# Reciprocal row sums of the first batch spread over 64 rows by TensorE transposes, and x of a pair formed one iteration sooner

## The chip, the cores and the metric

The kernel runs on one core of a Trainium2 chip. The metric is the device time of one execution in microseconds (us): the median of the runs. Before the change it is 807.39 us, the median of three runs from 806.12 to 808.97. For this kernel a difference of about 0.3% (2.4 us) is the least that can be told from no change.

## What is computed

The reference chains three blocks in float32: causal attention (4 batches, 12 heads, 448 tokens, 64 numbers per head), a gated block with a causal convolution of 5 taps, and a block with sine and cosine.

```python
scores = scale * q @ k.T ; masked above the diagonal
attn   = exp(scores - max)
attn   = attn / (attn.sum(-1) + 1e-9)
x      = attn @ v                         # heads side by side: (4, 448, 768)

gate   = 1 / (1 + exp(-conv5(x, conv_w)))
x      = (gate * (x @ w_val)) @ w_out

theta  = x @ w_theta
y      = w_tok_r @ (x * cos(theta)) + w_tok_i @ (x * sin(theta))
u      = x + y
out    = u + max(u @ w_ch, 0)
```

## The kernel before

**Attention, one iteration per head.** `attn_iter(i)` runs head i in five segments; two heads are a pair g, and each batch has six pairs. An iteration computes the scores of four row blocks (L320, L321: "S"), the row maxima on VectorE (L322), the exponentials on ScalarE (L116, with the row sums as a by-product), and in the iteration after it the transposes of the probabilities (L341) and their copies out of PSUM (L354). After both heads of a pair, TensorE multiplies by v (L364: "AV"), without having divided by the row sums. At the end of every odd iteration q and k of the next pair are transposed (L283) and split into a high and a low half (L298 to L308). No S of the next pair can start before these splits: below, this stretch is the boundary between two pairs.

**The division.** `attn_R` forms the reciprocals of the row sums, a tile `rec` of 112 rows x 8 (L379, L380). They are needed along the columns and equal on all 64 rows of a head. So `rec` is written to memory (`rows<-rec`, L382), and two DMAs read it back, each spreading a head's 448 numbers over 64 rows (`rb<-rows`, L397). All of these are issued from SyncE's queue, in order with every other load and store. `attn_X1` then forms x of the pair on VectorE, `xf = av * rb` (L408), splits it on ScalarE (`x_hi`, L413) and on GpSimd (`x_lo`, L108), and `attn_X2` runs the convolution (L423 to L430 on GpSimd) and the gate. In iterations, pair g is attended in 2g and 2g+1, its AV and its read-back stand at the end of iteration 2g+2, and `attn_X(g)` stands near the end of iteration 2g+3.

**The first batch.** There is no dense work beside the attention of batch 0. Its loop (L664) runs 69 segments: batch 0 and nearly two heads of batch 1. Beside it run the preparation of the first weight tiles (`to_f32` on VectorE: L153, L156, L160; splits on GpSimd: L105, L108) and, for two output tiles, the first dense product ahead of time: `gemm_ahead(kc)`, six 448-column matmuls per pair (L451), which reads `x_hi` and `x_lo` of pair kc. After it, `dense(b)` is interleaved with the attention of the next batch by a table of rates (L694 to L699).

**What sets the order.** Each engine runs its own list in order; a waiting instruction holds all behind it. A scheduler with a model of the times made the lists when the program was built. PSUM has 2 buffers for dense products and 6 for all else. `issue_after` keeps `xf` behind the last row maximum that was written before it in the code.

```python
seg(n): if j == 1 and n == (X_LAST if g == NP else X_SEG): attn_X(g - 1)   # L617, both 3
...
if AHEAD and i >= 4 and i % 2 == 0 and c == A_SEG and i // 2 - 2 < KC - 1:  # L678
    gemm_ahead(i // 2 - 2)
```

Of the kernel before, what the change touches and what calls it, by code (L numbers as in the profile page):

```python
# [9 lines left out]
F32 = mybir.dt.float32  # L10
# [11 lines left out]
ROUND = 12582912.0  # L22

X_SEG = 3
X_LAST = 3
U_DVE = (0, 1, 1, 1)
PT_DVE = (2, 2, 0, 0)
K_DUP = (2, 2, 2, 2, 2, 2, 0, 0, 0, 0, 0, 0, 0, 0, 0, 1, 0, 1, 0, 0, 0, 0, 0, 0)
# [5 lines left out]
AHEAD = 2  # L34
A_SEG = 2
# [14 lines left out]
def kernel(  # L50
# [14 lines left out]
    nc = tc.nc  # L65
    B, H, S, D = q.shape
    DM = H * D
    P = 128
    CP = 112
    NC = S // CP  # L70
    NP = H // 2
    KC = DM // P
# [8 lines left out]
    pool = ctx.enter_context(tc.tile_pool(name="pool", bufs=2))  # L81
# [18 lines left out]
    def psum(tag):  # L100
        at = "mm" if tag == "mm" else "at"
        return ps.tile([P, 512], F32, tag=at, name=f"ps_{tag}", bufs=2 if tag == "mm" else 6)
# [145 lines left out]
    gates = {}  # L248
    rbs = {}
    row_at = {}  # L250
    ttr_ins = []
    hf_ins = []

# [103 lines left out]
    def attn_AV(g):  # L357
        if not 0 <= g < B * NP:
            return
        tv = v_raw.pop(g)  # L360
        av[g] = psum("av")
        for kc in range(NC):
            for j in range(2):
                nc.tensor.matmul(  # L364
                    av[g][j * D : (j + 1) * D, kc * CP : S], lhsT=tv[:, j, kc, :], rhs=pT.pop((2 * g + j, kc)),
                    start=kc == 0, stop=kc == NC - 1, skip_group_check=True,
                )

    def attn_X(g):
        if not 0 <= g < B * NP:  # L370
            return
        attn_X1(g)
        attn_X2(g)

    def attn_R(g):
        if not 0 <= g < B * NP:
            return
        rec = pool.tile([CP, 2, NC], F32, tag="rec", name="rec")
        nc.vector.tensor_scalar(out=rec, in0=sums[g], scalar1=1.0e-9, scalar2=None, op0=ALU.add)  # L379
        nc.vector.reciprocal(rec, rec)  # L380
        rows = dram.tile([2, NC, CP], F32, tag="rows", name="rows", bufs=2)
        nc.sync.dma_start(out=rows.rearrange("h c p -> p h c"), in_=rec)  # L382
        row_at[g] = rows

    def attn_B(g):
        if g not in row_at:
            return
        rows = row_at.pop(g)
        with ExitStack() as st:
            if g + 2 in v_ins:  # L390
                st.enter_context(tc.issue_after(v_ins[g + 2].ins))
            attn_B2(g, rows)
# [50 lines left out]
    def gemm_ahead(kc):  # L443
        xhi, xlo = x_hl[0, kc]
        g = kc // KH
        for n in range(AHEAD):
            if kc == 0:
                ahead[n] = psum("mm" if n < 2 else "tr")
            whi, wlo = splits[n, g]
            for m, (a, x) in enumerate(((whi, xhi), (whi, xlo), (wlo, xhi))):  # L450
                nc.tensor.matmul(  # L451
                    ahead[n][:, :S], lhsT=a[:, kc % KH, :], rhs=x,
                    start=kc == 0 and m == 0, stop=kc == KC - 1 and m == 2, skip_group_check=True,
                )
            if kc == KC - 1:
                splits.pop((n, 0)), splits.pop((n, 1))
# [156 lines left out]
    def attn_iter(i):  # L613
        g, j = divmod(i, 2)

        def seg(n):
            if j == 1 and n == (X_LAST if g == NP else X_SEG):  # L617
                attn_X(g - 1)

        attn_PT(i - 1, (0,))  # L620
        attn_S(i, 0)
        seg(0)
        yield
        attn_PT(i - 1, (1,))
        attn_S(i, 1)
        seg(1)
        yield
        attn_PT(i - 1, (2, 3))
        attn_S(i, 2)
        seg(2)  # L630
        yield
        attn_S(i, 3)
        attn_T(i + 1)
        if j == 1:
            load_qk(g + 3, "q")
            load_qk(g + 3, "k")
            attn_R(g)
        seg(3)
        yield
        if j == 0:  # L640
            attn_AV(g - 1)
            load_v(g + 1)
            attn_B(g - 1)
        if i == B * H:
            attn_X(g - 1)
        seg(4)
        yield
# [16 lines left out]
    for n in range(5 * (H + 1) + X_SEG + 1):  # L664
        next(at, None)
        if n == 5:
            setup_conv()
        if W_AT <= n < 5 * H:
            with tc.issue_after(ttr_ins[-1].ins):
                for at_n, (m, g) in zip(A_TILES, ((0, 0), (1, 0), (0, 1), (1, 1), (2, 0), (2, 1), (3, 0), (3, 1))):  # L670
                    if n == at_n - W_AT:
                        load_w(m, g)
                    if n == at_n:
                        stage_w(m, g)
                        if m < AHEAD + 1:
                            split_w(m, g)
        i, c = divmod(n, 5)
        if AHEAD and i >= 4 and i % 2 == 0 and c == A_SEG and i // 2 - 2 < KC - 1:  # L678
            gemm_ahead(i // 2 - 2)
        if n == 5 * H - 3:  # L680
            with tc.issue_after(ttr_ins[-1].ins):
                for g in range(2):
                    load_w(AHEAD + 2, g)
    if AHEAD:
        gemm_ahead(KC - 1)
    for b in range(B):
        done = 0
        for y, _ in enumerate(dense(b)):
# [44 lines left out]
```

## Time and profile before

| | |
|---|---|
| median of 3 runs | 807.39 us |
| profiled execution, whole | 811.03 us |
| its span, first to last instruction | 809.2 us |
| TensorE busy | 725.1 us, 90% |
| VectorE busy | 493.8 us, 61% |
| ScalarE busy | 427.4 us, 53% |
| GpSimd busy | 316.2 us, 39% |
| mean granted TensorE clock | 0.949 of 2.4 GHz |

These are means over stages that differ. The attention of batch 0 by itself lasts to about 122 us; there no engine is busy throughout, and the TensorE clock is granted at its lower level (0.50: 1.2 GHz) for part of the time. From 122 to about 262 us VectorE is nearly always busy, and after that TensorE is. So the profile is read stage by stage.

### The profile page before, as it was taken

The page shows a single profiled execution, that of the slowest core. Times are in us where ns is not written, and L with a number is a line of the kernel's source. Part 1 is how long each engine was busy: PE and PEld are TensorE (multiplying, and loading weights), DVE is VectorE, ACT ScalarE, POOL GpSimd, SP SyncE. Part 2 cuts the span into 40 slices and gives each one's busy share as a digit, 9 for nine tenths or more (in the row PEclk, how much of TensorE's full clock was granted, in tenths as well). Part 3 has the DMA queues.
Part 4 walks back from the last instruction along what each step waited for, and adds up shares of the span by engine and source line. Part 5 has one row for each costly group of instructions (what it writes and reads, how often), then busy time and mean ns, then how long its engine had stood idle before and what let it go on. Part 6 is the DMA issues. An engine that isn't in the chain of part 4 may idle for free.

```text
span 809.2 us, 11956 instructions
## 1 busy us (share of the span) xinstructions
PE 725.1 (90%) x3965; PEld 609.7 (75%) x3965; DVE 493.8 (61%) x1125; ACT 427.4 (53%) x998; POOL 316.2 (39%) x327
## 2 busy tenths in 40 slices
PE   5687889698598798999989899899999998999997
PEld 4455558577387686788978788788888787988996
DVE  4666869999999837535657645653666732114541
ACT  6767754465567744435687633444787622124401
POOL 0386976586355658123226610113234232201100
PEclk9888779789699999999999999999999999999999
DMA  9548627979576248778744259579824078774323
GB/s 233 125 104 182 151 47 200 236 238 294 142 221 140 63 133 225 225 234 184 157 136 86 60 144 190 148 221 196 178 58 102 12 140 215 214 212 139 98 57 90
DMA packets 151850, 126.01 MB, mean 156 GB/s; under 512 B 93519, under 2 KB 126829, under 8 KB 151789
## 3 DMA queue, kind: packets, MB, share of 16 engines
q1 hardware_dynamic: 151789, 125.25, 60.9%
q8 instruction: 31, 0.51, 0.3%
q14 instruction: 30, 0.25, 0.1%
HBM read 100.76 MB, written 24.47 MB: 155 GB/s over the span
## 4 chain that ended last, share of the span: by engine, by line
PE 54%; DVE 18%; DMA 9%; ACT 8%; POOL 6%; issue 4%; SPq 1%; ACTq 0%; POOLq 0%; DVEq 0%
PE ps_mm L472 28%; PE ps_mm L567 10%; PE ps_av L364 5%; PE ps_tr L341 3%; PE ps_s L320 2%; DVE gate L434 2%; PE ps_s L321 2%; DMA out_dram<-o 2%; DVE cv_raw L156 2%; DMA rb<-rows 2%; DMA scratch<-w_hl 2%; POOL gate L430 2%; DVE qs L111 1%; DMA rows<-rec 1%; ACT prob L116 1%
## 5 line engine op out<-in xcount | busy, mean ns | idle before, releaser
L472 PE MATMUL ps_mm<-act_hi,w_hl 128*128 128x448 f32 x864 | 274.1, 379 | 10.7 <-POOL w_hl L105 7.0
L472 PEld LDWEIGHTS ps_mm<-act_hi,w_hl 128*128 128x128 f32 x864 | 165.1, 193 | 27.9 <-POOL w_hl L105 9.4
L472 PE MATMUL ps_mm<-act_lo,w_hl 128*128 128x448 f32 x432 | 160.4, 373 | 0.0
L116 ACT ACTIVATE prob<-ps_s,negm 112x112 f32<-112x112 f32 x192 | 95.4, 498 | 71.4 <-DVE negm L322 69.4
L322 DVE CUSTOM_DVE_ANT_0 ps_s<-ps_s,mask 112x112 f32<-112x112 f32 x192 | 86.2, 454 | 76.3 <-PE ps_s L321 62.6
L320 PE MATMUL ps_s<-kk,qs 128*112 128x256 f32 x192 | 73.9, 389 | 21.3 <-DVE qs L111 4.8
L341 PE MATMUL ps_tr<-ident,prob 112*112 112x112 f32 x480 | 80.4, 271 | 13.2 <-ACT prob L116 7.6
L108 POOL TENSOR_TENSOR act_lo<-x2f,act_hi 128x448 fp32r<-128x448 f32 x36 | 43.9, 1218 | 119.8 <-ACT act_hi L486 57.0
L472 PEld LDWEIGHTS ps_mm<-act_lo,w_hl 128*128 128x128 f32 x432 | 83.4, 194 | 5.0
L354 ACT COPY pt<-ps_tr 112x448 f32<-112x448 f32 (+2 forms) x120 | 51.5, 440 | 60.7 <-PE ps_tr L341 60.2
L472 PE MATMUL ps_mm<-x_hi,w_hl 128*128 128x448 f32 x264 | 80.5, 374 | 2.3 <-ACT x_hi L413 1.1
L341 PEld LDWEIGHTS ps_tr<-ident,prob 112*112 112x112 f32 x480 | 57.3, 138 | 28.0 <-ACT prob L116 11.7
L567 PE MATMUL ps_mm<-wtok_h,zt_h 128*128 128x448 f32 x168 | 64.2, 382 | 5.6 <-ACT zt_h L558 5.6
L567 PE MATMUL ps_mm<-wtok_h,zt_l 128*128 128x448 f32 x168 | 63.6, 378 | 1.3 <-DVE zt_l L111 1.1
L321 PE MATMUL ps_s<-klo,qs 128*112 128x256 f32 x192 | 63.0, 339 | 1.4 <-DVE klo L111 1.4
L364 PE MATMUL ps_av<-pt,v_raw 112*64 112x224 f32 (+3 forms) x384 | 63.3, 446 | 0.9 <-ACT prob L116 0.8
L567 PE MATMUL ps_mm<-wtok_l,zt_h 128*128 128x448 f32 x168 | 62.3, 371 | 0.0
L320 PEld LDWEIGHTS ps_s<-kk,qs 128*112 128x112 f32 x192 | 36.6, 192 | 30.0 <-ACT kk L307 6.5
L430 POOL TENSOR_TENSOR gate<-gate,tp 128x448 f32<-128x448 f32 x48 | 57.8, 1205 | 2.8
L108 POOL TENSOR_TENSOR x_lo<-xf,x_hi 128x448 fp32r<-128x448 f32 x23 | 29.4, 1279 | 74.5 <-ACT x_hi L413 74.1
L543 POOL TENSOR_TENSOR z<-z,x2f 128x448 f32<-128x448 f32 x18 | 20.9, 1160 | 92.3 <-ACT z L540 92.3
L472 PEld LDWEIGHTS ps_mm<-x_hi,w_hl 128*128 128x128 f32 x264 | 50.3, 191 | 8.6 <-DVE hf L510 2.2
(97 smaller groups left out, 1362.0 us busy)
## 6 DMA issues: line engine op xcount, KB each, us to landing
w_hl<-scratch SPq DMA_DIRECT2D x144, 384.0 KB, 3.9
scratch<-w_hl SPq DMA_DIRECT2D x44, 384.0 KB, 4.2
q_raw<-in_q_dram SPq DMA_DIRECT2D x48, 112.0 KB, 3.6
k_raw<-in_k_dram SPq DMA_DIRECT2D x48, 112.0 KB, 3.3
v_raw<-in_v_dram SPq DMA_DIRECT2D x24, 224.0 KB, 3.9
rb<-rows SPq DMA_DIRECT2D x48, 112.0 KB, 3.9
out_dram<-o SPq DMA_DIRECT2D x24, 224.0 KB, 3.8
cv_raw<-in_moe_w_val_dram SPq DMA_DIRECT2D x12, 384.0 KB, 6.3
```

What stands on the lines that cost most here:

```text
L108: nc.gpsimd.tensor_tensor(out=dst, in0=src, in1=f32(hi), op=ALU.subtract)
L116: exps.append(nc.scalar.activation(*args, **kw))
L320: nc.tensor.matmul(pt[:CP, :nn], lhsT=qs[:, cs], rhs=kk[:, :nn], start=True, stop=False)
L321: nc.tensor.matmul(pt[:CP, :nn], lhsT=qs[:, cs], rhs=klo[:, :nn], start=False, stop=True)
L322: ttr = nc.vector.tensor_tensor_reduce(out=pt[:CP, :n], in0=pt[:CP, :n], in1=mask[:, S - n : S], scale=-1.0 / math.sqrt(D), scalar=3.0e38, ...
L341: nc.tensor.transpose(pt[:CP, off : off + CP], prob[i, c][:, kc * CP : (kc + 1) * CP], ident[:CP, :CP])
L354: nc.scalar.copy(t, src)
L364: nc.tensor.matmul(av[g][j * D : (j + 1) * D, kc * CP : S], lhsT=tv[:, j, kc, :], rhs=pT.pop((2 * g + j, kc)), start=kc == 0, stop=kc == N ...
L430: nc.gpsimd.tensor_tensor(out=gt, in0=gt, in1=tp, op=ALU.add)
L472: nc.tensor.matmul(pt[:, :S], lhsT=a[:, kc % KH, :], rhs=x, start=kc == 0 and m == 0, stop=kc == KC - 1 and m == 2,)
L543: (nc.vector if Z_DVE[b] else nc.gpsimd).tensor_tensor(out=t, in0=t, in1=x2f[e], op=ALU.mult)
L567: nc.tensor.matmul(pt[:, :S], lhsT=a[:, m, :], rhs=w[:, m, :], start=m == 0 and n == 0, stop=m == NZ - 1 and n == 2,)
```

## The change

The reciprocals of the pairs of batch 0 no longer go through memory. VectorE copies `rec` into a tile `wide` in which each number stands 64 times (112 x 512); TensorE transposes its four blocks into a PSUM buffer, after which each head's 448 numbers lie along the columns on all 64 rows; ScalarE copies that to `rb`. The six `rows` writes and twelve `rb` reads of batch 0 are gone; the other batches keep theirs. `attn_X` of these pairs now stands right behind their AV, at the end of iteration 2g+2, and `gemm_ahead` moves from the even iterations to the odd ones, so that each comes an iteration sooner, the last inside the loop and not behind it.

```diff
-X_LAST = 3
+    wides = {}
 ...
         nc.vector.reciprocal(rec, rec)
+        if g < NP:
+            wide = pool.tile([CP, NC, 2, D], F32, tag="m2k", name="wide", bufs=2)
+            nc.vector.tensor_copy(wide, rec.rearrange("p h c -> p c h").unsqueeze(3).broadcast_to((CP, NC, 2, D)))
+            wides[g] = wide
+            return
         rows = dram.tile([2, NC, CP], F32, tag="rows", name="rows", bufs=2)
 ...
+    def attn_W(g):
+        wide = wides.pop(g)
+        rbs[g] = psum("tr")
+        for c in range(NC):
+            nc.tensor.transpose(
+                rbs[g][:, c * CP : (c + 1) * CP], wide[:, c].rearrange("p h d -> p (h d)"), ident[:CP, :CP]
+            )
+        rb = pool.tile([P, S], F32, tag="m2k", name="rb", bufs=2)
+        nc.scalar.copy(rb, rbs[g][:, :S])
+        rbs[g] = rb
 ...
-            if j == 1 and n == (X_LAST if g == NP else X_SEG):
+            if j == 1 and g > NP and n == X_SEG:
                 attn_X(g - 1)
 ...
         if j == 0:
+            if g - 1 in wides:
+                attn_W(g - 1)
             attn_AV(g - 1)
             load_v(g + 1)
             attn_B(g - 1)
+            if 1 <= g <= NP:
+                attn_X(g - 1)
 ...
-        if AHEAD and i >= 4 and i % 2 == 0 and c == A_SEG and i // 2 - 2 < KC - 1:
-            gemm_ahead(i // 2 - 2)
+        if AHEAD and i >= 3 and i % 2 == 1 and c == A_SEG:
+            gemm_ahead((i - 3) // 2)
 ...
-    if AHEAD:
-        gemm_ahead(KC - 1)
```

On VectorE, around the product `xf` of the first pair (`xf_72`; ISA is the row maximum, `qs` and `klo` the low halves of q and k of the next pair), the list before reads:

```order
L322 ISA ps_s,negm<-ps_s,mask 112x448
L322 ISA negm 112x1
L352 COPY pt<-ps_tr 112x112
L111 TENSOR_TENSOR qs<-ps_tr,qs 64x448
L379 TENSOR_SCALAR rec<-sums 112x8
L408 TENSOR_TENSOR xf_72<-ps_av,rb 128x448
L380 RECIPROCAL rec<-rec 112x8
L111 TENSOR_TENSOR klo_74<-ps_tr,kk 64x448
L111 TENSOR_TENSOR qs<-ps_tr,qs 64x448
```

and after the change, with the same `xf` in the middle of the iteration and the new copy in the old place:

```order
L322 ISA ps_s,negm<-ps_s,mask 112x112
L322 ISA negm 112x1
L424 TENSOR_TENSOR xf_72<-ps_av,rb 128x448
L322 ISA ps_s,negm<-ps_s,mask 112x224
L322 ISA negm 112x1
L159 SCALAR_TENSOR_TENSOR cv_raw<-cv_raw 128x384
```

```order
L379 TENSOR_SCALAR rec<-sums 112x8
L380 RECIPROCAL rec<-rec 112x8
L383 COPY wide<-rec 112x512
L110 TENSOR_TENSOR klo_74<-ps_tr,kk 64x448
```

So `xf` has left the boundary, and a copy of 512 columns has come into it, ahead of the low halves.

On TensorE, at the boundary behind the third pair of heads, the list before has the six ahead-of-time matmuls (L451; two are seen here, four follow behind AV) behind the first S of the next pair:

```order
L283 MATMUL ps_tr<-ident,q_raw 128x112 x4
L283 MATMUL ps_tr<-ident,k_raw 128x112 x4
L341 MATMUL ps_tr<-ident,prob 112x112 x4
L320 MATMUL ps_s<-kk,qs 112x256
L341 MATMUL ps_tr<-ident,prob 112x112 x3
L320 MATMUL ps_s<-kk,qs 112x256
L321 MATMUL ps_s<-klo_74,qs 112x256 x2
L341 MATMUL ps_tr<-ident,prob 112x112 x3
L451 MATMUL ps_mm<-x_hi,w_ahead 128x448 x2
```

and after the change ahead of it (L467):

```order
L283 MATMUL ps_tr<-ident,q_raw 128x112 x4
L283 MATMUL ps_tr<-ident,k_raw 128x112 x4
L467 MATMUL ps_mm<-x_hi,w_ahead 128x448 x2
L341 MATMUL ps_tr<-ident,prob 112x112 x4
L467 MATMUL ps_mm<-x_lo,w_ahead 128x448
L467 MATMUL ps_mm<-x_hi,w_ahead 128x448
L467 MATMUL ps_mm<-x_lo,w_ahead 128x448
L467 MATMUL ps_mm<-x_hi,w_ahead 128x448
L320 MATMUL ps_s<-kk,qs 112x256
```

All six now stand between the transposes of q and k and the first S.

On GpSimd, for the second pair (`xf_73`), the list after the change puts a weight tile's low half between the first convolution steps and `x_lo`:

```order
L439 TENSOR_SCALAR gate<-xf_73,cw 128x448
L443 TENSOR_SCALAR tp<-xf_73,cw 128x448
L107 TENSOR_TENSOR w_ahead<-cv_raw,w_ahead 128x384
L446 TENSOR_TENSOR gate<-gate,tp 128x448
L107 TENSOR_TENSOR x_lo<-xf_73,x_hi 128x448
```

As before, `x_lo` is not the first of the GpSimd instructions that follow an `xf`.

## Rows read from the trace of the kernel before

**Rows 1.** Windows, us: busy PE, PEld, DVE, ACT, POOL; granted clock, DMA share
```profile
31.00:113.00 82.00, 65.10 (x332) 43.79 (x333) 57.76 (x157) 57.21 (x160) 59.68 (x66) 0.81 0.61 139
113.00:122.00 9.00, 8.35 (x34) 5.17 (x34) 5.14 (x15) 4.70 (x14) 8.30 (x11) 0.62 0.07 2
122.00:162.00 40.00, 32.57 (x156) 26.94 (x152) 38.27 (x73) 18.47 (x41) 23.83 (x21) 0.86 0.87 221
...
202.00:262.00 60.00, 46.64 (x243) 37.90 (x243) 56.44 (x117) 37.31 (x79) 28.07 (x28) 0.89 0.65 170
```

**Rows 2.** Chain that ended last, 15 to 70 us: start, length, what
```profile
19.53 11.37 DMA rows<-rec
...
32.10 3.19 DMA rb<-rows
...
35.31 0.64 DVE xf L408
...
35.99 0.55 PE ps_s L320
```

**Rows 3.** The tile rb to 130 us: instructions, and waits before them (us, times)
```profile
L408 DVE TENSOR_TENSOR xf<-ps_av,rb x6: 611/624/625, 35.3 to 111.5; 128x448 f32<-128x448 f32 x6
...
  DMA rb<-rows: 8.1, 5
```

**Rows 4.** Timeline of VectorE: start, length, instruction, idle before and its releaser
```profile
21.64 0.36 DVE L153 TENSOR_SCALAR cv_raw<-cv_raw 128x384 int32<-128x384 uint32 x1
...
35.31 0.62 DVE L408 TENSOR_TENSOR xf<-ps_av,rb 128x448 f32<-128x448 f32 x1 [4.16 <-DMA rb<-rows]
...
111.48 0.62 DVE L408 TENSOR_TENSOR xf<-ps_av,rb 128x448 f32<-128x448 f32 x1 [2.07 <-DMA rb<-rows]
...
121.47 0.62 DVE L510 SCALAR_TENSOR_TENSOR hf<-gate,ps_mm 128x448 f32<-128x448 f32 x1 [2.92 <-PE ps_mm L451]
```

**Rows 5.** Timeline of TensorE: transposes of q, AV, boundary, ahead-of-time matmuls
```profile
16.51 0.95 PE L283 MATMUL ps_tr<-ident,q_raw 112*128 112x112 f32 x4
...
28.37 0.55 PE L283 MATMUL ps_tr<-ident,q_raw 112*128 112x112 f32 x4
...
44.39 0.41 PE L364 MATMUL ps_av<-pt,v_raw 112*64 112x112 f32 x2
...
48.50 0.31 PE L341 MATMUL ps_tr<-ident,prob 112*112 112x112 f32 x1 [0.51 <-ACT prob L116]
49.45 0.37 PE L320 MATMUL ps_s<-kk,qs 128*112 128x256 f32 x1 [0.64 <-DVE rec L379]
...
59.74 0.36 PE L451 MATMUL ps_mm<-x_hi,w_ahead 128*128 128x448 f32 x1
59.94 0.37 PE L451 MATMUL ps_mm<-x_lo,w_ahead 128*128 128x448 f32 x1
```

**Rows 6.** Windows around one boundary: the granted clock stands behind the five engines
```profile
48.00:52.00 4.00, 2.12 (x11) 1.31 (x11) 3.59 (x11) 3.91 (x9) 1.47 (x2) 0.97 0.85 201
52.00:56.00 4.00, 3.94 (x10) 2.04 (x12) 3.15 (x10) 3.50 (x12) 4.00 (x5) 0.50 0.16 51
```

**Rows 7.** Timeline of ScalarE: a copy of 448 columns out of PSUM
```profile
98.04 0.53 ACT L354 COPY pt<-ps_tr 112x448 f32<-112x448 f32 x1
```

**Rows 8.** Chain that ended last, 0 to 260 us: its longest transfer behind the loop
```profile
207.92 6.45 DMA cv_raw<-in_moe_w_theta_dram
```

**Rows 9.** Timeline of GpSimd: convolution, low halves, a slow step
```profile
54.10 1.01 POOL L108 TENSOR_TENSOR w_ahead<-cv_raw,w_ahead 128x384 fp32r<-128x384 f32 x1
...
64.76 0.64 POOL L423 TENSOR_SCALAR gate<-xf,cw 128x448 f32<-128x448 f32 x1 [1.08 <-DVE xf L408]
...
66.11 1.14 POOL L430 TENSOR_TENSOR gate<-gate,tp 128x448 f32<-128x448 f32 x1
67.20 1.14 POOL L108 TENSOR_TENSOR x_lo<-xf,x_hi 128x448 fp32r<-128x448 f32 x1
...
88.95 2.15 POOL L430 TENSOR_TENSOR gate<-gate,tp 128x448 f32<-128x448 f32 x1
```

## The prediction

> **What bounds the kernel now.** I read the windows by stage first, since the change touches batch 0 alone. In the attention loop, taken from 31 to 113 us, no engine is full: TensorE is busy 65.1 us, VectorE 57.8, GpSimd 59.7, and the granted clock is 0.81 [rows 1]. That loop is bound by latency, by who waits for whom in turn. From 122 to 262 us VectorE is nearly full, 38.3 of 40 us at its start and 56.4 of 60 at its end: there VectorE is the bound, and when that stage starts decides when it ends [rows 1]. The lists of all engines read alike again from the middle of the program on, so I expect nothing of the change there but an earlier start.
>
> Second I read the chain that ended last. In the loop it runs through the read-back of the reciprocals: 11.37 us for the write of the first `rec`, 3.19 us for the read, then `xf`, then S of the next pair [rows 2]. Third, what `xf` waited for: in five of six pairs VectorE stood idle for the read-back, 8.1 us together [rows 3], the longest waits 4.16 and 2.07 us, so the other three have 1.9 us between them [rows 4]. VectorE's list is in order, and behind `xf` stand the low halves of q and k and the row maxima that S and the exponentials of the next pair need: in the chain `xf` runs from 35.31 for 0.64 us and S follows at 35.99 [rows 2]. Last, the boundary. TensorE idles there in pieces (0.51 and 0.64 us are shown) [rows 5], is busy 2.12 of 4 us at a clock of 0.97, and in the next window is busy throughout at 0.50, the 1.2 GHz level [rows 6]. So after a boundary the same matmuls take about twice as long, and this repeats pair by pair (`xf` of the six pairs starts from 35.3 to 111.5 us, every 15.2 us [rows 3]): a mean of 0.81 over 82 us is (1 - 0.81) x 2 x 82 = 31 us at the lower level.
>
> **The change part by part.** The profiled execution took 811.03 us, 3.64 us over the median of 807.39; I sum the differences against 811.03 and carry the sum to the median.
>
> *Waits removed.* The new `xf` needs AV and `rb`, both of which TensorE has just produced, and stands between two row maxima. The two long waits go whole: nothing else is late there, since the splits of q and k that follow had their inputs. Of the short three I count half, because TensorE waits at these boundaries for ScalarE's copies too. 4.16 + 2.07 + 0.9 = 7.1 us. Bounds: 4.2 (only the longest counts) to 8.1. Taken: -7.1.
>
> *SyncE's queue.* Six writes and twelve reads leave it. What stood behind them (q, k, v, weights) moves earlier, but v still waits for AV; I cost it at nothing.
>
> *Ahead-of-time matmuls moved.* Six matmuls of 448 columns per pair go from behind the first S, where the clock is often low, into the boundary. At the higher clock they follow each other in 0.20 us (59.74 to 59.94) [rows 5], so six take 1.2 us, and the boundary shown has 0.51 + 0.64 = 1.15 us of idle TensorE to take them. A whole cover would save 1.2 us a pair at full clock, 2.4 at half; none would cost 1.2 us a pair ahead of S instead. I take 0.7 us for each of five pairs, since two of the six need `x_lo`, which is last to come. Bounds: -12 to +3. Taken: -3.5.
>
> *Clock.* 31 us at the lower level, if TensorE was the bound throughout, cost half of that, 15.6 us. With six real matmuls in the boundary some drops will come later or not at all, but the waits for ScalarE and VectorE between them remain. Bounds: -15.6 to 0. Taken: -2.5, nearer to none, as the boundary shown lost the clock with pieces of idle time of well under 1 us [rows 5, 6].
>
> The Trainium skill (TensorE: Matmul & The Clock Gate, Part 4: PE-mode transpose) says that transposes do not count as activity for the clock in the way matmuls do. The boundary agrees: TensorE was busy there, by the profile, mostly with transposes, and the clock fell. By that rule the 24 added transposes hold no clock, and only the six moved matmuls can; that is one more reason for a small share.
>
> *Added.* TensorE: six times four transposes of the very shape of L283, 0.55 us for four at the higher clock and 0.95 at the lower [rows 5]: 3.3 to 5.7 us, in front of AV, in order, so all on the path. Taken 3.3. VectorE: six copies of 512 columns from SBUF to SBUF, not seen before. Nearest are 0.36 us for 384 columns with both ends in SBUF and 0.62 us for a product of 448 [rows 4]: 2.2 to 3.7 us, or by columns 0.48 each, 2.9. The copy stands in the boundary ahead of the low halves; half of it lies beside ScalarE's copies, which the low halves wait for. Taken 1.5. ScalarE: six copies of 448 columns at 0.53 us [rows 7], 3.2 us, among the exponentials; ScalarE is idle 25 of 82 us [rows 1], so I take 1.2. Together +6.0, bounds +1.5 to +12.6.
>
> *Tail.* The last ahead-of-time product now stands inside the loop. Before, VectorE waited 2.92 us for it with its first gated product [rows 4] in a stretch where VectorE was busy 5.1 of 9 us [rows 1]. The weight and token work behind it, which bounds the next 140 us, can start sooner. Next late is the score work of the two heads of batch 1, which has to be done all the same. Taken -1.5, bounds -2.9 to 0.
>
> *Given back.* In the stage bound by VectorE the chain has transfers of its own, the longest 6.45 us [rows 8], and the lists there are shuffled too. They move with the stage, since their buffers come free with it; I take +1.2, bounds 0 to +8.
>
> Sum: -7.1 - 3.5 - 2.5 + 6.0 - 1.5 + 1.2 = -7.4. 811.03 - 7.4 = 803.6 for an execution like the profiled one; against the median, 807.39 - 7.4 = **800.0 us**.
>
> **Rivals.**
>
> *x_lo holds TensorE (slower).* Four of the six matmuls stand ahead of S behind one that reads `x_lo`, in order. GpSimd makes `x_lo` behind other work: for the second pair two steps of 0.64, a weight's low half of 1.01, a step of 1.14 and `x_lo` itself, 1.14 [rows 9], 4.6 us behind `xf`. AV of that pair ended at 44.8 us (44.39 + 0.41), so with `xf` at 45.4 `x_lo` comes at 50.0, when S had started at 49.45 [rows 5]; S would be some 1.4 us later by 0.6 of waiting and four matmuls. For pairs without the weight step it is 3.6 us and in time. Against the rival: only one or two pairs look like this. For it: GpSimd is the busiest engine but TensorE in the loop, and a step of 1.14 us took 2.15 in a crowded place [rows 9]. It decides if S is held over 1.5 us at each boundary. At 2.5 us for each of five it costs 12.5: 800.0 + 12.5 = 812.5 us, a loss.
>
> The Trainium skill (SBUF — State Buffer, Who interferes with whom) says that a VectorE copy with both ends in SBUF can take the port pair it shares with GpSimd, and that the later of the two then waits for the whole instruction. The slow GpSimd step of 2.15 us ran beside VectorE's weight work and agrees. By that rule each new copy can hold GpSimd for its own length, an estimate of 0.48 us from the row above, just ahead of the boundary's matmuls: some 3 us more over six pairs in this rival, none in the forecast.
>
> *Given back whole.* The loop ends sooner, but the stage bound by VectorE waits for transfers (DMA share 0.87 in 122 to 162 us [rows 1]) and takes most of it back: the +8 bound in place of +1.2, 800.0 + 6.8 = 806.8 us, no change. For it, the transfer in the chain; against it, that VectorE is 96% busy in the same stretch, so it rarely waits.
>
> *The clock holds.* With the matmuls in the boundary the drops do not come: 15.6 in place of 2.5 us, 800.0 - 13.1 = 786.9 us. For it, the idle pieces that the matmuls fill are the greater part of what TensorE lacked; against it, the waits for the exponentials stay.
>
> **How the numbers follow.** The forecast 0.53, with a range of its own from 795 to 805; x_lo 0.16; given back 0.17; the clock 0.14. Faster by over 0.3% (under 805.0) has nearly all of the forecast and the clock, and a little of the given-back case: 0.69. Within 0.3%, which is about what a measurement of this kernel can tell from no change: 0.16. Slower (over 809.8): 0.15. The range from 789 to 809 leaves out the deeper half of the clock case and most of the x_lo case, 2 in 10 together.
>
> **What would show it.** Right: no idle time before `xf` put down to a DMA up to 120 us; intervals between the `xf` nearer 14 than 15.2 us; the first gated product (121.47 before) some 6 to 9 us sooner; the same shift still there at 262 us. The clock term shows in the mean granted clock from 31 us to the end of the loop, 0.81 before: above 0.9 would speak for the clock case. Wrong: TensorE's first S behind a boundary waiting for `x_lo`, or ahead-of-time matmuls waiting long in front of it; VectorE's idle time growing between 122 and 262 us; `xf` waiting for AV as long as it did for the DMA.

## The result, and the profile after

The changed kernel takes 796.97 us (median of 4 runs, 795.86 to 799.73); the kernel before took 808.18 beside it (4 runs, 806.12 to 812.58). The ratio is 0.9859, with an interval from 0.981 to 0.9908: 11.2 us faster. The profiled execution of the changed kernel took 796.42 us, with a span of 794.6 us and a mean granted clock of 0.976; against that of before, 811.03 us, it is 14.6 us shorter, 3.4 us more than the medians differ.

The windows by stage of the changed kernel, with the columns of [rows 1]:

```profile
31.00:113.00 82.00, 68.26 (x411) 48.83 (x413) 74.04 (x182) 64.94 (x181) 70.66 (x78) 0.96 0.45 119
113.00:122.00 9.00, 8.23 (x50) 6.75 (x47) 8.24 (x18) 4.39 (x11) 7.37 (x7) 1.00 0.89 288
122.00:162.00 40.00, 28.18 (x141) 22.11 (x141) 39.78 (x73) 21.41 (x50) 20.90 (x21) 0.91 0.84 226
...
202.00:262.00 60.00, 47.71 (x275) 40.28 (x275) 55.21 (x111) 40.43 (x86) 31.65 (x32) 0.97 0.67 168
```

The granted clock in the loop rose from 0.81 to 0.96, and VectorE did 74.0 us of work there in place of 57.8. From 122 us on VectorE is about as full as before. So the loop now does more in the same 82 us, and the next stage still has the same bound.

The tile `wide` to 130 us, and then the tile `xf`, to be read against [rows 3] (name, count, then shortest, median and longest in ns, and first and last start):

```profile
L394 PE MATMUL ps_tr<-ident,wide x24: 257/260/394, 23.7 to 94.3; 112*128 112x112 f32 x24
L383 DVE COPY wide<-rec x6: 427/709/1160, 19.3 to 92.1; 112x512 f32<-112x512 f32 x6
```

```profile
L424 DVE TENSOR_TENSOR xf<-ps_av,rb x6: 611/622/625, 28.1 to 98.9; 128x448 f32<-128x448 f32 x6
```

The six `xf` run from 28.1 to 98.9 us, one every 14.2 us, where it was 15.2. No idle time stands before any of them, for a DMA or for AV. The copy took 709 ns at the median, not the 480 that I worked out by columns.

The waits show where VectorE's time came from. First its groups up to 132 us of the kernel before (count, busy us, mean ns, then the idle time before them and what ended it), and after it those of the changed kernel:

```profile
L322 DVE CUSTOM_DVE_ANT_0 ps_s<-ps_s,mask 112x112 f32<-112x112 f32 (+3 forms) x62 | 27.6, 455 | 16.6 <-PE ps_s L321 13.2 <-PE ps_tr L341 1.2 <-ACT pt L354 1.1
...
L156 DVE SCALAR_TENSOR_TENSOR cv_raw<-cv_raw 128x384 int32<-128x384 int32 (+1 forms) x13 | 8.8, 680 | 0.2
```

```profile
L322 DVE CUSTOM_DVE_ANT_0 ps_s<-ps_s,mask 112x112 f32<-112x112 f32 (+3 forms) x62 | 27.1, 456 | 4.6 <-PE ps_s L321 4.0 <-PE ps_tr L341 0.2
L155 DVE SCALAR_TENSOR_TENSOR cv_raw<-cv_raw 128x384 int32<-128x384 int32 (+1 forms) x16 | 13.3, 829 | 0.1
...
L383 DVE COPY wide<-rec 112x512 f32<-112x512 f32 x6 | 4.6, 760 | 0.2
```

Before the same 62 row maxima VectorE idles 4.6 us, where it idled 16.6; the scores (L321) ended 4.0 us of this, where they ended 13.2. In the time won VectorE does more of the weight work, 16 steps of L155 in place of 13, but each takes 829 ns in place of 680. The whole of VectorE up to 132 us and behind it, by windows of before and then of after:

```profile
0.00:132.00 132.00, 103.37 (x528) 72.34 (x529) 89.83 (x248) 88.02 (x243) 79.21 (x94) 0.84 0.60 136
132.00:262.00 130.00, 105.65 (x533) 86.36 (x533) 125.00 (x242) 74.48 (x164) 76.07 (x73) 0.88 0.80 221
```

```profile
0.00:132.00 132.00, 106.13 (x607) 77.72 (x607) 110.94 (x277) 94.41 (x257) 88.77 (x101) 0.96 0.62 165
132.00:262.00 130.00, 100.32 (x532) 81.53 (x531) 124.64 (x243) 79.81 (x181) 72.06 (x74) 0.95 0.73 191
```

By 132 us VectorE has 110.9 us of work behind it in place of 89.8: 21.1 us more. Behind that it is full in both. Over the whole span its work grew from 493.8 to 503.7 us, by 9.9. What is left is 21.1 - 9.9 = 11.2 us. The first `z` of batch 0, a landmark inside that stage, comes 11.8 us sooner (first and last start stand behind the durations; before, then after):

```profile
L528 DVE TENSOR_SCALAR z<-z x24: 375/386/1170, 204.7 to 766.2; 128x448 f32<-128x448 f32 x24
```

```profile
L544 DVE TENSOR_SCALAR z<-z x24: 380/388/1225, 192.9 to 751.4; 128x448 f32<-128x448 f32 x24
```

The timeline of TensorE at the boundary behind the third pair, which [rows 5, 6] show for before; first two more lines of before, the transposes of q at this boundary and at the next, and then the changed kernel:

```profile
46.45 0.55 PE L283 MATMUL ps_tr<-ident,q_raw 112*128 112x112 f32 x4
...
61.97 0.55 PE L283 MATMUL ps_tr<-ident,q_raw 112*128 112x112 f32 x4
```

```profile
42.92 0.55 PE L283 MATMUL ps_tr<-ident,q_raw 112*128 112x112 f32 x4
...
43.66 0.67 PE L467 MATMUL ps_mm<-x_hi,w_ahead 128*128 128x448 f32 x2
45.25 0.70 PE L341 MATMUL ps_tr<-ident,prob 112*112 112x112 f32 x4 [0.93 <-DVE pt L352]
47.38 0.47 PE L467 MATMUL ps_mm<-x_lo,w_ahead 128*128 128x448 f32 x1 [1.43 <-POOL x_lo L107]
47.68 0.36 PE L467 MATMUL ps_mm<-x_hi,w_ahead 128*128 128x448 f32 x1
47.88 0.37 PE L467 MATMUL ps_mm<-x_lo,w_ahead 128*128 128x448 f32 x1
48.09 0.36 PE L467 MATMUL ps_mm<-x_hi,w_ahead 128*128 128x448 f32 x1
48.29 0.28 PE L320 MATMUL ps_s<-kk,qs 128*112 128x256 f32 x1
...
51.52 0.55 PE L394 MATMUL ps_tr<-ident,wide 112*128 112x112 f32 x4
...
57.17 0.55 PE L283 MATMUL ps_tr<-ident,q_raw 112*128 112x112 f32 x4
```

and the windows there, with the granted clock behind the five engines, and one from later in the loop:

```profile
44.00:48.00 4.00, 1.65 (x9) 1.01 (x8) 3.87 (x7) 3.91 (x11) 3.94 (x4) 1.00 0.64 164
48.00:52.00 4.00, 3.13 (x22) 2.31 (x20) 3.88 (x10) 2.26 (x7) 3.46 (x5) 1.00 0.14 49
52.00:56.00 4.00, 4.00 (x27) 2.16 (x27) 3.37 (x11) 3.40 (x11) 3.30 (x4) 1.00 0.17 53
...
80.00:84.00 4.00, 4.00 (x18) 1.96 (x17) 3.91 (x8) 2.15 (x8) 3.16 (x3) 0.54 0.25 98
```

The wait for `x_lo` of the first rival is there, 1.43 us at its longest, 3.7 us over five boundaries. And this boundary became longer: from the transposes of q to the first S it takes 5.37 us (42.92 to 48.29), where it took 3.00 (46.45 to 49.45). What became shorter is the stretch behind it, from this S to the next transposes of q: 8.88 us (to 57.17) in place of 12.52 (to 61.97). There the clock, which fell to 0.50 at this place before, stays at 1.00. It does not hold everywhere: behind the fifth pair TensorE had its six matmuls too, but then waited 1.29 and 2.31 us for `qs`, and the clock fell, to 0.54 on average from 80 to 84 us.

Last, the end of the loop: the first gated product, before at 121.47 us with 2.92 us of waiting [rows 4], in the changed kernel's timeline of VectorE:

```profile
102.82 0.62 DVE L526 SCALAR_TENSOR_TENSOR hf<-gate,ps_mm 128x448 f32<-128x448 f32 x1 [1.30 <-PE ps_mm L467]
103.36 0.50 DVE L379 TENSOR_SCALAR rec<-sums 112x8 f32<-112x8 f32 x1
```

and the same `rec`, that of the first two heads of batch 1, before:

```profile
112.96 0.52 DVE L379 TENSOR_SCALAR rec<-sums 112x8 f32<-112x8 f32 x1
```

The gated product is 18.7 us sooner, but it also passed this `rec` in the list. The score work itself is 9.6 us ahead.

### The profile page after: what moved, and what is told of

Same layout as the page of the kernel before. It is cut to its first block, busy times and chain, and to the rows that moved or that the text cites. A ratio compares the mean times of both kernels' runs of the same rounds, so it can differ in the third digit from the quotient of the medians.

```text
span 794.6 us, 11969 instructions
## 1 busy us (share of the span) xinstructions
PE 713.9 (90%) x3989; PEld 603.9 (76%) x3989; DVE 503.7 (63%) x1131; ACT 429.3 (54%) x1004; POOL 314.4 (40%) x327
## 4 chain that ended last, share of the span: by engine, by line
PE 52%; DVE 22%; DMA 9%; ACT 8%; POOL 4%; issue 3%; SPq 0%; ACTq 0%; DVEq 0%; POOLq 0%
PE ps_mm L488 28%; PE ps_mm L583 10%; DMA out_dram<-o 4%; PE ps_av L364 4%; PE ps_tr L341 3%; DVE cv_raw L155 3%; DVE ps_s L322 2%; DVE cv_raw L159 2%; PE ps_s L320 2%; DVE gate L450 2%; PE ps_s L321 2%; DVE qs L110 2%; DVE cv_raw L152 2%; ACT prob L115 2%; PE ps_tr L569 1%
## 5 line engine op out<-in xcount | busy, mean ns | idle before, releaser
L320 PE MATMUL ps_s<-kk,qs 128*112 128x256 f32 x192 | 71.2, 374 | 18.9 <-DVE qs L110 7.2
L341 PE MATMUL ps_tr<-ident,prob 112*112 112x112 f32 x480 | 78.7, 269 | 6.2 <-ACT prob L115 3.2
L321 PE MATMUL ps_s<-klo,qs 128*112 128x256 f32 x192 | 60.4, 326 | 1.8 <-DVE klo L110 1.8
L364 PE MATMUL ps_av<-pt,v_raw 112*64 112x448 f32 (+3 forms) x384 | 58.7, 419 | 0.4 <-ACT prob L115 0.4
L320 PEld LDWEIGHTS ps_s<-kk,qs 128*112 128x112 f32 x192 | 34.8, 183 | 27.3 <-DVE qs L110 5.0
```

Source lines behind the costliest of these rows:

```text
L320: nc.tensor.matmul(pt[:CP, :nn], lhsT=qs[:, cs], rhs=kk[:, :nn], start=True, stop=False)
L321: nc.tensor.matmul(pt[:CP, :nn], lhsT=qs[:, cs], rhs=klo[:, :nn], start=False, stop=True)
L341: nc.tensor.transpose(pt[:CP, off : off + CP], prob[i, c][:, kc * CP : (kc + 1) * CP], ident[:CP, :CP])
L364: nc.tensor.matmul(av[g][j * D : (j + 1) * D, kc * CP : S], lhsT=tv[:, j, kc, :], rhs=pT.pop((2 * g + j, kc)), start=kc == 0, stop=kc == N ...
```

## The experiments

The theory was: the read-back is gone, VectorE no longer stalls in the boundary, and that makes most of the gain. The rival was: x comes sooner, TensorE has real matmuls in the boundary, and the clock that they hold makes it. A third question was why an advance of 18.7 us at the end of the loop was worth 11 to 15. Each kernel is compared with the kernel before on the same chip.

### The two parts apart

**The new route with x at its old place.** `attn_X` and the ahead-of-time products stand where they stood before.

```diff
-            if j == 1 and g > NP and n == X_SEG:
+            if j == 1 and n == X_SEG:
                 attn_X(g - 1)
 ...
-            if 1 <= g <= NP:
-                attn_X(g - 1)
 ...
-        if AHEAD and i >= 3 and i % 2 == 1 and c == A_SEG:
-            gemm_ahead((i - 3) // 2)
+        if AHEAD and i >= 4 and i % 2 == 0 and c == A_SEG and i // 2 - 2 < KC - 1:
+            gemm_ahead(i // 2 - 2)
 ...
+    if AHEAD:
+        gemm_ahead(KC - 1)
```

> The reciprocals of batch 0 go through TensorE, but x and the ahead-of-time products stand where they stood before the change. Waits theory (the gain is the read-back that xf no longer waits for): most of the 11 us stays, 797 to 800 us, and no wait of xf for a DMA before 120 us. Clock theory (the gain is that the six matmuls stand in the boundary and TensorE's clock no longer falls): the waits go, the copies and transposes are paid, the clock still falls at each boundary (mean granted clock of 31 to 113 us near 0.81 as before); 803 to 808 us.

801.18 us (794.95 to 801.95) against 809.31; ratio 0.9875 (0.9824 to 0.9925). Its window of the loop and VectorE's largest wait up to 132 us:

```profile
31.00:113.00 82.00, 69.84 (x371) 51.43 (x373) 67.69 (x175) 63.09 (x178) 64.25 (x71) 0.80 0.42 113
```

```profile
DVE ps_s L322 <- PE ps_s L321: 9.5, 12, 2.6
```

The clock is as low as before, no `xf` waits for a DMA, and most of the gain is there: 8.1 us, with the interval from 6.1 to 14.2, where the next kernel, on the same chip, gains 11.5. The time lies between the ranges of the two theories, nearer to that of the waits. So the route by itself pays, without the clock. It takes the eighteen small transfers out of SyncE's queue as well, which was not tried apart; VectorE's waits for other transfers up to 132 us are 1.4 us here and 1.5 before, so none of the gain is seen there.

**x sooner, products at their old lines.** Only the last two pieces of the diff above.

> The change, but the ahead-of-time products stand at their old places, an iteration later, the last behind the loop; x is formed early as in the change. Clock theory: the boundary loses its matmuls, the clock falls to the 1.2 GHz level behind most boundaries again, 802 to 807 us, and VectorE's wait for the first gated product returns. Waits theory: the read-back is gone all the same, 796 to 800 us.

797.85 us (793.32 to 801.63), ratio 0.9848 (0.979 to 0.9906). The scheduler made the same lists as for the change, so this is a repeat of it and tells one thing: the moved lines of `gemm_ahead` do nothing by themselves. The products go where x allows; `attn_X` is what moved them.

**The new order with the read-back kept.**

```diff
-        if g < NP:
+        if g < 0:
             wide = pool.tile([CP, NC, 2, D], F32, tag="m2k", name="wide", bufs=2)
```

> The order of the change with the old route: rec is written to memory and read back, x and the products stand an iteration sooner. If the order alone brings the gain, 796 to 800 us. If the route is what makes the order possible, xf now waits in the middle of the iteration for 8 us of write and 3.4 us of read, less what the iteration before covers: I expect 2 to 5 us of wait for each of six pairs, 812 to 830 us, slower than before.

808.88 us (802.48 to 810.44, 10 runs) against 809.31; ratio 0.9983 (0.9958 to 1.0008): no difference. The wait of `xf`, from the view of the tile `rb`:

```profile
  DMA rb<-rows: 6.5, 3
```

The profiled execution was the fastest of the ten, 802.48 us. The read-back still holds `xf`, x comes too late for the boundary, the products fall behind the first S again, and the clock in the loop is 0.82. I had expected a loss; the read-back only costs what it cost before. No gain of the new order is seen without the route.

### The clock apart

**Products held behind S.** The change, with each pair's ahead-of-time products kept behind the third S of the next pair.

```diff
-        nc.tensor.matmul(pt[:CP, :nn], lhsT=qs[:, cs], rhs=klo[:, :nn], start=False, stop=True)
+        s_ins.append(nc.tensor.matmul(pt[:CP, :nn], lhsT=qs[:, cs], rhs=klo[:, :nn], start=False, stop=True))
 ...
-        if AHEAD and i >= 3 and i % 2 == 1 and c == A_SEG:
-            gemm_ahead((i - 3) // 2)
+        if AHEAD and i >= 4 and i % 2 == 0 and c == A_SEG and i // 2 - 2 < KC - 1:
+            with tc.issue_after(s_ins[-1].ins):
+                gemm_ahead(i // 2 - 2)
 ...
+    if AHEAD:
+        gemm_ahead(KC - 1)
```

> The change, with the ahead-of-time products held behind the third S of the next pair, where they mostly stood before; x is formed early as in the change. (In the run with the late products the scheduler had made the very lists of the change, so that one was only a repeat of it.) Clock theory: the boundary is empty again, the granted clock of 31 to 100 us falls from 0.95 to 0.8, and the time rises to 800 to 804 us. Waits theory: no wait comes back, the S of the next pair no longer stands behind x_lo, and the time is that of the change or better, 793 to 798 us.

801.0 us (800.13 to 804.78) against 810.4; ratio 0.9894 (0.986 to 0.9928). TensorE at the same boundary, and windows of it and of the loop to 100 us:

```profile
46.42 0.31 PE L342 MATMUL ps_tr<-ident,prob 112*112 112x112 f32 x1 [0.70 <-ACT prob L115]
47.83 0.42 PE L321 MATMUL ps_s<-kk,qs 128*112 128x256 f32 x1 [1.09 <-DVE qs L110]
```

```profile
44.00:48.00 4.00, 1.86 (x14) 1.32 (x14) 3.68 (x7) 3.94 (x13) 3.82 (x4) 0.99 0.64 161
48.00:52.00 4.00, 3.40 (x14) 3.07 (x14) 3.62 (x11) 3.40 (x10) 2.55 (x5) 0.50 0.13 46
...
31.00:100.00 69.00, 53.51 (x294) 39.82 (x295) 55.24 (x144) 51.12 (x144) 55.51 (x61) 0.82 0.46 127
```

S starts at 47.83, even sooner than with the change, but the clock falls to 0.50 behind the boundary, where it stayed at 1.00. TensorE was busy a little longer here from 44 to 48 us than with the change, 1.86 us in place of 1.65, but nearly all of it with transposes. All four runs are slower than every run of the version with the copy on ScalarE (below) on the same chip, 794.78 to 797.96. Against the ratios of the change (0.9859, 0.9848 and 0.9873 in three comparisons) it loses 2 to 4 us. The intervals touch, so the size is not sharper than that. VectorE waits here for two things for which it does not wait with the change:

```profile
DVE xf L425 <- PE ps_av L365: 4.0, 2, 2.2
DVE cv_raw L152 <- DMA cv_raw<-in_moe_w_val_dram: 3.3, 1, 3.3
```

The first fits a TensorE at half its rate, the second is a weight's transfer. Holding the products also moves them in front of the fourth S. So the loss is that of the clock and of the new order together, not parted here.

**A filled boundary before the change.** The kernel before, with six matmuls of 448 columns, whose product nothing reads, added behind the transposes of q and k at the ends of the third to the sixth pair; they take the high half of x of two pairs back.

```diff
+        if j == 1 and 2 <= g < NP:
+            xh = x_hl[0, g - 2][0]
+            dummy = psum("tr")
+            with tc.issue_after(t_ins[-1].ins):
+                for m in range(6):
+                    nc.tensor.matmul(dummy[:, :S], lhsT=xh[:, 0:P], rhs=xh, start=m == 0, stop=m == 5)
```

> The kernel before, with six more matmuls of 448 columns in four of the boundaries (pairs 2 to 5), whose result nobody reads; all else as before, the wait for the read-back too. Clock theory: the added work pays for itself, granted clock of 31 to 113 us above 0.85 (0.81 before), 803 to 808 us, not slower than before. If what TensorE does in the boundary is not what holds the clock: the clock stays near 0.81 and the time is that of before or up to 8 us more, 808 to 817 us.

808.38 us (805.92 to 812.51) against 810.4; ratio 0.9982 (0.9943 to 1.002). The loop's window, and the wait of `xf`:

```profile
31.00:113.00 82.00, 63.60 (x359) 45.30 (x359) 60.56 (x162) 59.25 (x165) 60.15 (x68) 0.88 0.61 140
```

```profile
  DMA rb<-rows: 7.0, 4
```

The first of the four groups of added matmuls:

```profile
46.33 1.49 PE L640 MATMUL ps_tr<-x_hi 128*128 128x448 f32 x6
```

Behind three of the four filled boundaries (matmuls at 46.33, 60.80 and 93.42 us) the clock stays at 1.00. At the remaining one the six came at 77.91, after 4.34 us without work for TensorE, and the clock fell to 0.50, as it did at the two boundaries that were left unfilled, near 34 and 111 us. So the added matmuls kept the clock up in this kernel where they came in time. That raised the loop's clock from 0.81 to 0.88, as the clock theory had it (above 0.85), but the time is just outside its range and not shown to differ from that of before. The reason is open: `xf` still waits for its read-back, and the added matmuls take 7.05 us of TensorE in the boundaries themselves.

### The copy and the low half

**The copy made twice.**

```diff
             nc.vector.tensor_copy(wide, rec.rearrange("p h c -> p c h").unsqueeze(3).broadcast_to((CP, NC, 2, D)))
+            nc.vector.tensor_copy(wide, rec.rearrange("p h c -> p c h").unsqueeze(3).broadcast_to((CP, NC, 2, D)))
```

> The change with VectorE's copy of the reciprocals made twice, so that its price is seen once more: six copies of about 0.7 us. If VectorE's time in the loop is covered by the waits at the boundary: within 1 us of the change, 797 to 798 us. If VectorE is on the path there (it did 111 of the first 132 us in the change, 90 before): 4 us more, 800 to 803 us.

803.66 us (799.56 to 805.54) against 809.31; ratio 0.9906 (0.9872 to 0.994). The second copies, the loop, and a wait that the change does not have:

```profile
L384 DVE COPY wide<-rec x6: 420/508/828, 20.8 to 105.1; 112x512 f32<-112x512 f32 x6
```

```profile
31.00:113.00 82.00, 62.31 (x341) 42.34 (x341) 65.66 (x162) 56.08 (x160) 57.19 (x66) 0.83 0.40 110
```

```profile
DVE xf L425 <- PE ps_av L364: 3.3, 3, 2.0
```

On the same chip it is 5.8 us slower than the kernel with the lists of the change (797.85 us; the single runs of the two overlap), but the clock fell too and `xf` came to wait, so it does not price a copy by itself.

**The copy on ScalarE**, and in the last comparison again, beside the change:

```diff
-            nc.vector.tensor_copy(wide, rec.rearrange("p h c -> p c h").unsqueeze(3).broadcast_to((CP, NC, 2, D)))
+            nc.scalar.copy(wide, rec.rearrange("p h c -> p c h").unsqueeze(3).broadcast_to((CP, NC, 2, D)))
```

> The change with the copy of the reciprocals to 512 columns on ScalarE and not on VectorE. The copy made twice on VectorE cost 6 us, so VectorE is on the path there. If the price is VectorE's time: 4 to 6 us sooner, 791 to 794 us. If any engine pays the same at the boundary, since ScalarE makes the splits of q and k there: within 2 us of the change, 795 to 799 us.

> The change with the copy of the reciprocals on ScalarE, once more beside the change. If VectorE's time is what the copy costs: 2 to 5 us under the change, 793 to 796 us. If the copy costs the same on either engine: within 1.5 us of the change.

796.57 us (794.78 to 797.96), ratio 0.9829 (0.98 to 0.9859); again 795.88 (791.05 to 798.39), 0.9863 (0.9832 to 0.9894). The copy there:

```profile
L383 ACT COPY wide<-rec x6: 617/618/621, 20.6 to 91.7; 112x512 f32<-112x512 f32 x6
```

**The change again**, on the chip of the last comparison:

> The change itself, once more, on the same chip as the three below, so that small steps can be compared: 796 to 799 us, some 11 us under before.

796.17 us (790.95 to 799.61) against 806.36; 0.9873 (0.9838 to 0.9909). Beside it the copy on ScalarE is the same. In its first profile VectorE is relieved of 4.6 us and has done 106.4 us by 132 us in place of 110.9. Either the copy lay in time in which VectorE would otherwise have idled, or it costs as much on ScalarE; these runs do not tell which.

**x_lo on VectorE**, for batch 0, with the change's copy:

```diff
-        (dve_lo if X_LO[g] else pool_lo)(lo, x[:, PAD:], hi)
+        (dve_lo if X_LO[g] or g < NP else pool_lo)(lo, x[:, PAD:], hi)
```

> The change with x_lo of batch 0 on VectorE and not on GpSimd. In the change TensorE waits some 4 to 5 us in front of the products for x_lo from GpSimd. If that wait is on the path: 3 us sooner, 793 to 796 us. If VectorE is the bound of the loop by now: six products of 0.62 us more on it, 798 to 802 us.

798.94 us (797.02 to 800.97), ratio 0.986 (0.9827 to 0.9894): no gain. The clock in the loop was 0.90 here, so it is no test of VectorE's time alone.

**The copy on ScalarE with x_lo made sooner:** once ahead of one of the first two convolution steps on GpSimd (an order kept by `issue_after`; the other step, L447, still stands before it in the trace), once on VectorE as above.

> The copy on ScalarE, and on GpSimd x_lo of batch 0 ahead of the first step of the convolution. If TensorE's wait for x_lo (4 to 5 us in the change, 2 with the copy on ScalarE) is on the path: 1 to 2 us under the run with the copy on ScalarE alone. If the clock and VectorE decide: the same within 1 us.

> The copy on ScalarE and x_lo of batch 0 on VectorE, which takes about as much VectorE time as the copy left free and frees GpSimd of six steps of 1.14 us. If VectorE is the bound of the loop: like the change or up to 2 us over it, 796 to 800 us. If x_lo's lateness is: 1 to 3 us under the run with the copy on ScalarE alone.

795.17 us (793.02 to 798.82), 0.9882 (0.9857 to 0.9908), and 795.14 (790.67 to 796.99), 0.9856 (0.9828 to 0.9884). With `x_lo` ahead of that step, TensorE's wait for it is this:

```profile
  PE ps_mm L471: 0.7, 3
```

That is not clearly shorter than without the edit: with the copy on ScalarE alone it was 1.3 us in three places, and 0.4 in two in the last comparison. It is the copy's move that shortened it, from 3.7 us with the change (4.2 in the change again), and that brought no time. All four kernels of that comparison lie within 1.1 us of each other, so none is shown to be better than the change.

### The experiments together

What VectorE has done by 132 us, beyond the 89.83 of before, less what its work grew over the whole span, against the first `z`; all from one profiled execution of each, and beside them what the medians gained against before on the same chip. Differences were taken before rounding.

| kernel | clock 31 to 113 | idle before the maxima by 132, us | VectorE ahead by 132, us | its growth, us | net, us | first `z` sooner, us | by the medians, us |
|---|---|---|---|---|---|---|---|
| before | 0.81 | 16.6 | | | | | |
| read-back kept, new order | 0.82 | 12.7 | 6.5 | 4.3 | 2.2 | 4.8 | 0.4 |
| filled boundary | 0.88 | 12.7 | 3.6 | -1.9 | 5.5 | 2.1 | 2.0 |
| copy twice | 0.83 | 9.6 | 12.6 | 12.4 | 0.2 | 2.0 | 5.6 |
| route only | 0.80 | 13.9 | 11.6 | 4.5 | 7.1 | 8.1 | 8.1 |
| products held | 0.83 | 9.1 | 9.4 | 1.0 | 8.4 | 7.5 | 9.4 |
| the change | 0.96 | 4.6 | 21.1 | 9.9 | 11.2 | 11.8 | 11.2 |
| the same lists, products at their old lines | 0.96 | 3.8 | 21.6 | 9.7 | 12.0 | 12.1 | 11.5 |
| the change again | 0.98 | 3.7 | 23.3 | 10.1 | 13.3 | 13.6 | 10.2 |
| x_lo on VectorE | 0.90 | 6.8 | 19.8 | 10.3 | 9.5 | 11.7 | 11.5 |
| copy on ScalarE | 0.96 | 5.4 | 16.6 | 5.3 | 11.3 | 12.3 | 13.8 |
| copy on ScalarE again | 0.94 | 6.4 | 13.1 | 3.8 | 9.3 | 9.9 | 10.5 |
| the same, x_lo sooner | 0.96 | 4.5 | 16.3 | 5.1 | 11.2 | 13.5 | 11.2 |
| the same, x_lo on VectorE | 0.94 | 5.0 | 17.7 | 4.1 | 13.5 | 15.4 | 11.2 |

The net and the advance of `z` agree within 3.5 us in every row, and within 1 us for the change, its two repeats and the copy on ScalarE. That is bookkeeping more than proof: `z` starts after VectorE's work before it plus VectorE's idle time before it, 161.03 + 43.67 us before and 171.33 + 21.57 with the change. It says where the time went, not what made the idle time shorter. It works because VectorE has next to no idle time from 132 us to `z` (1.5 us before, 0.5 with the change; 3.1 in the filled boundary, whose row agrees least), so what counts is how much of its work it did before.

What made it shorter is told by the runs. The route alone brings 8.1 of 11.5 us on one chip (the single runs of the two overlap), the new order with the read-back brings nothing that shows, and the change without the products in the boundary, its clock nearly as low as before, loses 2 to 4 us. So the first theory has most of the gain, and the clock with the new order the rest. The idle time before the maxima goes with the clock only in part: the kernels of 0.90 and more have 3.7 to 6.8 us of it, the others 9.1 to 16.6, but of the 12.0 us that the change saved there 7.5 were saved with the products held too, at 0.83.

## Why the prediction was right, and what it sized wrongly

The direction and the reason held: the loop was bound by latency, the read-back was a part of it, and the following stage passed the gain on. I forecast -7.4 us; the medians differ by 11.2, the profiled pair by 14.6. The terms were mis-sized both ways, one group by too little gain and one by too much, and that the sum came as near as it did is in part luck. Term by term:

- **Waits removed, -7.1, and added, +6.0: mis-sized.** Route only has these two terms and neither the products nor the clock nor the tail, so the sum gives it -1.1 us; it measured -8.1, and -6.1 at the least. The step that failed is "in front of AV, in order, so all on the path", with 3.3 of the 6.0 us; the copies are the rest. The 8.1 us in front of `xf` are gone and no wait stands there in their place. Four transposes took 0.55 us at 51.52, as the row of before had it; the copies took 760 ns on average in place of 480, 4.6 us together, and on ScalarE they left the time as it was. Whether the added work cost nothing, or the read-back had cost more than its 8.1 us, is open: the runs measure the two together.
- **Products moved and clock, -3.5 and -2.5: the reasoning failed, and in time they were if anything too large.** The clock term was put "nearer to none, as the boundary shown lost the clock with pieces of idle time of well under 1 us". I took the idle pieces for the cause. The windows of the change show TensorE busy only 1.65 of 4 us with a clock of 1.00, and the unread matmuls put into the kernel before raised it to 0.88. At this boundary what stood in it, matmuls or transposes, mattered more than the gaps did; at the fifth the clock fell with the matmuls there, beside a gap of 2.31 us. The Trainium skill (TensorE: Matmul & The Clock Gate, Part 4: PE-mode transpose) says that transposes don't count as activity as matmuls do; the runs agree (0.50 behind a boundary of transposes, 1.00 behind the same one with six matmuls in it), and I had drawn too little from it. The price came out smaller than the 6.0 us of the two terms all the same: 2 to 4 us in products held, 3.3 between route only and x sooner, where the tail is included and the runs overlap. The bounds of the products were not worked out evenly: no cover, at 1.2 us a pair, is +6 for five pairs, not +3.
- **Tail, -1.5.** 2.92 us of waiting became 1.30: 1.6.
- **Given back, +1.2.** The stage itself did not take the gain back: 125.00 and 124.64 us of 130. But 5.3 us of VectorE's growth are in work that the change does not touch; L155 went from 680 to 829 ns on average up to 132 us. Why was not parted. GpSimd was busier beside it, 70.7 us of 82 in place of 59.7, but with the copy on ScalarE it was busier still, 74.0, and L155 took 700 ns.

VectorE's own account of the profiled pair is -8.1 before `xf`, -12.0 before the maxima, -1.6 before the gated product and +9.9 of work, -11.8 together, with 0.6 us of other waits on top: -11.2. That this is also the difference of the medians is chance; the pair itself differs by 14.6 us, of which 2.8 fall behind the first `z`.

**The rivals.** *The clock holds* happened as to its mechanism, 0.96 being above the 0.9 that I had named for it, but its price was wrong: 31 us at half the rate are not 15.6 us of time, since TensorE did not bound the loop throughout. On one chip, kernels with the route that differ in the clock lie 3.3 us apart (route only against x sooner, whose runs overlap) and 4.4 us (products held against the copy on ScalarE). *x_lo holds TensorE* was there as a wait, 3.7 us at five boundaries, longest 1.4 us, just under the 1.5 from which I had it decide, and the boundaries behind the third and the sixth pair took 5.4 and 4.9 us in place of 3.0 and 3.3; but with the copy on ScalarE the wait fell from 4.2 to 0.4 us in one comparison and the time stayed. The copies did not hold GpSimd by their length there: `x_lo` took 1122 to 1445 ns, before 1128 to 1152. *Given back whole* did not come.

**The signs that I had named.** No DMA before `xf`, and 14.2 us from one `xf` to the next: right. The first gated product 6 to 9 us sooner: it was 18.7, of which a part is only its new place ahead of `rec`, which came 9.6 us sooner. "The same shift still there at 262 us" was the wrong sign to choose, because it takes one instruction's place for the progress of an engine; VectorE's work done by a given time was the right one.

## What to carry to other kernels

In a loop bound by latency ahead of a stage bound by one engine, measure a change by how much of that engine's work is done when the stage begins, not by when one marked instruction starts: here 21.1 us less 9.9 of growth, where the instruction moved by 18.7. Such an account shows where time went; what each part of a change is worth still has to be run. Taking a round trip of a small tile through memory out of the loop brought 8.1 us here, about what VectorE had idled for it, though transposes and copies came in its place. Filling the gap with the round trip still in it showed no gain, at the price of matmuls that nothing used, so the wait is the first thing to try. When transposes are all that TensorE does in a gap, ask which real matmuls could stand there.

## What the runs showed that I had not expected

- With six matmuls of 448 columns among the transposes of the third boundary the granted clock stayed at 1.00 through a stretch in which TensorE was busy 1.65 of 4 us. Without them it fell to 0.50 at the same place, in the kernel before and with the products held. At the fifth boundary it fell with them too.
- All five boundaries behind the second to the sixth pair got longer with the change, that behind the third by 2.4 us. The time was won between them.
- The same copy of 112 x 512 took 427 to 1160 ns on VectorE, and 617 to 621 on ScalarE. Moved to ScalarE it gave no time back.
- Code that moved the ahead-of-time products left the lists as they were; only the readiness of x moved them.
